# A two-layer transformer on one core: 76 instead of 50 score tiles exponentiated on VectorE, and each engine's instruction order from a table

## The chip, the core and the metric

The kernel runs on one core of a Trainium2 chip. Its engines are TensorE (PE, with its weight loads shown apart as PEld), VectorE (DVE), ScalarE (ACT), GpSimd (POOL) and SyncE (SP, which issues the transfers). They run side by side, each through its own list of instructions in the order in which the program gives them; between engines only semaphores hold order. The metric is the device time of one execution in microseconds (us).

## What is computed

The input x has 2048 rows of 448 numbers in bfloat16. Two layers follow one another with the same weights. Each is an attention block with 16 heads of 28 and then a mixing block with a GELU MLP:

```python
def _A_ref(x, wqkv, wo):
    qkv = (x @ wqkv).reshape(B, S, 3, H, Dh).transpose(2, 0, 3, 1, 4)
    q, k, v = qkv[0], qkv[1], qkv[2]
    scores = jnp.einsum("bhqd,bhkd->bhqk", q, k) * (Dh ** -0.5)
    p = _softmax(scores, axis=-1)
    o = jnp.einsum("bhqk,bhkd->bhqd", p, v)
    return o.transpose(0, 2, 1, 3).reshape(B, S, D) @ wo
def _B_ref(x, w1, w2, w3, w4):
    h = _gelu(_layernorm(x) @ w1)
    # four quarters of h are shifted by 1, -1, 2 and -2 rows
    x1 = x + shifted(h) @ w2
    return x1 + _gelu(_layernorm(x1) @ w3) @ w4
x = A_x
x = x + _A_ref(_layernorm(x), A_wqkv, A_wo)
x = x + _B_ref(_layernorm(x), B_w1, B_w2, B_w3, B_w4)
# ... and both lines once more
```

## The kernel before, in words

**Tiles.** Rows go in 16 tiles of 128. Four heads share the 128 partitions (a head takes 32), so there are four head groups g. A unit u is a block of query rows (512; in the second layer's end also 256). A segment is a unit, a head group and a run of key tiles; `ORDER` (L545) and `UNITS` (L558) lay out 56 of them one after another. For each segment the scores are built transposed, keys on partitions: one score tile is 128 keys by 512 queries of one head and fills one of the eight PSUM banks.

**The exponentials.** Score tiles are put into 821 groups ("grans"), in turn of 3 and 2 tiles: 409 of three, 409 of two and 3 of one. Groups of three lie in banks 0 to 2 or, alternating, groups of two in banks 3 and 4; bank 5 accumulates P·V; banks 6 and 7 (and 0 to 4 outside the attention) serve the rest. For group n, `st_ops` (L1221) issues the score matmuls, four heads on four row strips of the array (L1243). One ACT instruction over all the group's tiles takes the exponential, from PSUM into the buffer `PT` (L1269). Then the matmuls of group n+2 may fill the same banks. `t_pv` (L1280) multiplies P by V, four heads on four column strips (L1318); a column of ones in V gives the softmax denominator. `t_norm` (L1333) takes the sum out of bank 5, in part through a scratch buffer in memory where a segment holds only part of the keys, and divides.

**Tiles on VectorE.** In 50 groups of three the third tile isn't in the ACT instruction: `t_dexp` (L1156) computes its exponential on VectorE in five instructions, by integer arithmetic on the floating-point bits and a cubic: L1159 reads the bank into the integer buffer `t32` (after it the bank is free, event `d1`, for which the third tile's matmul of group n+2 waits), L1166, L1167 and L1168 form the correction in the two halves of `gt`, and L1172 writes the result into one of three `PTD` slots. The PV matmuls of such a tile come up to `DEFER` = 4 key steps later than their neighbours. Which groups do so is said by `OFFL` (L512) and `on_dve` (L1132): every sixth or eighth index in six stretches, if the third tile lies neither in the first nor in the last three key steps of its segment.

**The rest of the work.** K, Q and V of a row chunk come from matmuls on a transposed, normalised copy (`kq_proj` L913, `v_proj` L974). The mixer's first matmul uses a GELU written through tanh, with VectorE before and after ScalarE (`tanh_gelu` L1404); its MLP stores 14 pieces, evacuated by VectorE (L1609), and takes the GELU in few large ACT instructions (L1650), each batch between two loads of ScalarE's function table. The last three tiles take the GELU straight from PSUM (L1606, L1488). A matmul with 128 output columns can be issued whole (L665) or as four of 32 (L668).

**What sets the order.** No order is written out by hand. Every piece of work is a Python generator that yields operations with an estimated duration; `Sched.run` (L319) plays them in a model of the engines, choosing at each step the candidate with the earliest start and the best rank, and appends it to its engine's list. Ranks come from `latest_starts` (L477) of the pass before. `ROUNDS` = 2 passes are followed by two that shift ranks at listed moments by seeded random numbers (`MOVES` L519, `perturb` L455). Where an operation has an alternative engine (`alt`), the model takes it if it ends earlier there, but gives ACT none while the attention runs (`reserve`). A load is modelled as a fixed time from its issue. `keep_pe_busy` (L291) puts filler matmuls on a matrix of ones (line L1686 of the profile) where the model has PE idle, up to 0.8 of a 4 us window. Banks and buffer slots are taken as the model reaches the operation. `Plan` (L47) turns shared buffers into semaphore waits.

Of the kernel before, what the change touches and what calls it, by code (L numbers as in the profile page):

```python
# [17 lines left out]
class _Op:  # L18
    __slots__ = ("eng", "fn", "deps", "sig", "cnt", "waits", "dma", "ekey", "vc", "sem", "t_end", "pos", "every", "oid", "dur", "lft", "lst")

    def __init__(self, eng, fn, dma):
# [16 lines left out]
        self.lst = None  # L38


def _split(acc):
    if isinstance(acc, tuple) and len(acc) == 2 and isinstance(acc[0], tuple):
        return acc
    return acc, None

# [122 lines left out]
class Sched:  # L168
# [8 lines left out]
    def __init__(self, P):  # L177
# [4 lines left out]
        self.pe_mode = None  # L182
        self.act_tab = None
# [8 lines left out]
        self.fill = None  # L192
        self.recent = []
        self.clock = 0.0
        self.plan = None
        self.moves = []
# [3 lines left out]
    def spawn(self, gen, prio=5, order=None, parent=None):  # L200
        self.seq += 1
        if parent is None:
            tid = (self.seq,)
        else:
            parent[7] += 1
            tid = parent[6] + (parent[7],)
        self.tasks.append([prio, self.seq if order is None else order + self.seq * 1e-6, gen, None, None, False, tid, 0, 0, None])

    def rank(self, t):
        if self.plan is None:  # L210
            return (t[0], t[1])
        return (self.plan.get((t[6], t[8]), 1e9), t[1])
# [4 lines left out]
    def _advance(self, t, force=False):  # L217
        changed = False
        while True:
# [39 lines left out]
            elif c == "acq":  # L259
# [22 lines left out]
                t[4] = got  # L282
# [8 lines left out]
    def keep_pe_busy(self, until):  # L291
        if self.fill is None:
            return
        dur, fn, banks, key, reads = self.fill
        while self.cur["pe"] + dur + 0.12 < until:
# [21 lines left out]
            self.pe_mode = "plain"  # L317

    def run(self):  # L319
        P = self.P  # L320
        while True:
            while self.moves and self.clock >= self.moves[0][0]:
                self.perturb(self.moves.pop(0)[1])
# [23 lines left out]
            for t in self.tasks:  # L347
# [5 lines left out]
                for a in kw0.get("alt", ()):  # L353
                    cands.append(a)
# [8 lines left out]
                for ci, (eng, dur, fn, kw) in enumerate(cands):  # L363
# [13 lines left out]
                    if ci > 0 and (self.cur[eng] > ready + 0.05 or eng in self.reserved):  # L377
                        continue
# [57 lines left out]
            op = P.add(eng, fn, reads, writes, kw.get("deps", ()), dma, t_end)  # L436
            self.live.update(k for k in (_split(a)[0] for a in writes) if k[0] == "ps")
            self.live.difference_update(kw.get("last", ()))
            op.oid = (t[6], t[8])
# [15 lines left out]
    def perturb(self, seed):  # L455
        rng = random.Random(seed)
        if rng.random() < 0.2:
            self.SLACK = rng.choice((0.0, 0.06, 0.12, 0.3))
            self.TOL = rng.choice((0.0, 0.5, 1.5, 4.0))
            self.EPS = rng.choice((0.02, 0.05, 0.12))  # L460
        t = self.clock - self.shift
        lo, hi = t - 30.0, t + rng.choice((10.0, 25.0, 50.0, 90.0))
# [1314 lines left out]
```

## Time and profile before

| | before |
|---|---|
| three runs | 1058.69 to 1058.89 us, median 1058.83 |
| profiled execution, first to last instruction | 1059.8 us |
| instructions in it | 22773 |
| first exponential starts, last one's stretch ends | 27.17 us, 1023.12 us |

The profiled execution is one of its own; nothing of it is known beside its span, which is 0.97 us above the median of the runs. A page of the profile gives for each engine the busy time and how many instructions it ran; then the chain of work that ended last, followed back from the last instruction; then groups of instructions, with the line, the engine, the operation, output<-input (partitions x elements and type), the count, and behind the first bar the busy time in us and the mean length of one in ns, behind the second the idle time of the engine just before them and what ended most of it. A row of waits reads: who waited, for whom, us in total, how many times, the longest. A row of windows reads: from:to, its length, busy us (and count) of PE, PEld, DVE, ACT and POOL, the TensorE clock that was granted, the busy share of the transfer engines, GB/s.

### The profile page before, as it was taken

The page shows a single profiled execution, that of the slowest core. Times are in us where ns is not written, and L with a number is a line of the kernel's source. Part 1 is how long each engine was busy: PE and PEld are TensorE (multiplying, and loading weights), DVE is VectorE, ACT ScalarE, POOL GpSimd, SP SyncE. Part 2 cuts the span into 40 slices and gives each one's busy share as a digit, 9 for nine tenths or more (in the row PEclk, how much of TensorE's full clock was granted, in tenths as well). Part 3 has the DMA queues.
Part 4 walks back from the last instruction along what each step waited for, and adds up shares of the span by engine and source line. Part 5 has one row for each costly group of instructions (what it writes and reads, how often), then busy time and mean ns, then how long its engine had stood idle before and what let it go on. Part 6 is the DMA issues. An engine that isn't in the chain of part 4 may idle for free.

```text
span 1059.8 us, 22773 instructions
## 1 busy us (share of the span) xinstructions
PE 1020.3 (96%) x9869; PEld 397.8 (38%) x9883; DVE 744.5 (70%) x1686; ACT 1015.2 (96%) x933; POOL 57.8 (5%) x80
## 2 busy tenths in 40 slices
PE   9999999999999999999999999989999999999998
PEld 5333332333333333333443443323333333434456
DVE  7966579866987547887689657785879645666454
ACT  5999999999999999999999999999999999999983
POOL 2000000100000001010101000000010000010000
PEclk8999999999999999999999999989999999999999
DMA  4243141001101002110111103211010100110000
GB/s 116 63 122 87 36 122 21 2 16 20 21 2 21 1 1 42 36 21 2 21 41 32 29 8 81 81 41 41 21 36 2 20 15 19 21 22 1 15 6 23
DMA packets 70717, 35.14 MB, mean 33 GB/s; under 512 B 56472, under 2 KB 65048, under 8 KB 70616
## 3 DMA queue, kind: packets, MB, share of 16 engines
q1 hardware_dynamic: 70616, 33.68, 13.4%
q8 instruction: 77, 1.26, 0.5%
q14 instruction: 24, 0.20, 0.1%
HBM read 12.70 MB, written 7.08 MB: 19 GB/s over the span
## 4 chain that ended last, share of the span: by engine, by line
ACT 52%; PE 41%; DVE 4%; DMA 1%; issue 1%; SPq 0%; POOLq 0%; POOL 0%; DVEq 0%
ACT PT L1269 45%; PE ps L1243 11%; PE ps L1318 9%; PE ps L665 9%; PE ps L1686 6%; ACT h2T L1650 4%; PE ps L916 3%; PE ps L668 3%; ACT gt L1433 1%; ACT L1650 1%; ACT L1269 1%; DVE kT L925 1%; DMA xT<-xn 1%; DMA wk_raw<-in_A_wqkv_dram 1%; DVE h2T L1609 0%
## 5 line engine op out<-in xcount | busy, mean ns | idle before, releaser
L1269 ACT ACTIVATE PT<-ps 128x1024 bf16<-128x1024 f32 (+1 forms) x821 | 917.2, 1225 | 10.2 <-PE ps L1243 6.4
L1243 PE MATMUL ps<-qT,kT 32*128 32x512 bf16 x1536 | 240.0, 386 | 13.8 <-ACT PT L1269 11.3
L1318 PE MATMUL ps<-PT,vaug 128*32 128x512 bf16 (+1 forms) x2253 | 250.0, 362 | 2.8 <-ACT PT L1269 1.4
L1686 PE MATMUL ps<-ones_bf 128*128 128x256 bf16 x928 | 143.6, 279 | 2.8 <-DVE hot L698 1.1
L1243 PEld LDWEIGHTS ps<-qT,kT 32*128 32x128 bf16 x1536 | 58.6, 91 | 196.1 <-ACT PT L1269 113.7
L665 PE MATMUL ps<-xT,w 112*128 112x512 bf16 (+5 forms) x623 | 129.2, 325 | 0.5 <-DVE h2T L1609 0.2
L1318 PEld LDWEIGHTS ps<-PT,vaug 128*32 128x32 bf16 x2253 | 65.7, 94 | 118.2 <-issue 66.0
L1609 DVE CAST h2T<-ps 128x512 bf16<-128x512 f32 (+2 forms) x126 | 73.5, 583 | 48.2 <-PE ps L665 40.3
L1686 PEld LDWEIGHTS ps<-ones_bf 128*128 128x128 bf16 x928 | 77.4, 99 | 71.3 <-issue 50.8
L1243 PE MATMUL ps<-kT 32*128 32x256 bf16 (+1 forms) x768 | 80.1, 310 | 2.5 <-ACT PT L1269 1.6
L665 PE MATMUL ps<-w,h2T 128*128 128x448 bf16 x327 | 75.1, 354 | 4.8 <-ACT h2T L1650 3.5
L665 PEld LDWEIGHTS ps<-xT,w 112*128 112x128 bf16 (+1 forms) x623 | 50.2, 103 | 53.6 <-issue 27.7
L1159 DVE TENSOR_SCALAR t<-ps 128x512 int32<-128x512 f32 x50 | 34.2, 684 | 34.4 <-PE ps L1243 34.0
L668 PE MATMUL ps<-xT,w 112*32 112x512 bf16 (+4 forms) x612 | 51.5, 337 | 0.0
L916 PE MATMUL ps<-xT,wq_raw 112*32 112x512 bf16 (+1 forms) x576 | 46.8, 367 | 1.9 <-DVE kT L925 0.9
L1243 PEld LDWEIGHTS ps<-kT 32*128 32x128 bf16 x768 | 21.4, 91 | 64.1 <-ACT PT L1269 32.8
L1650 ACT ACTIVATE h2T<-h2T 128x7168 bf16<-128x7168 bf16 (+2 forms) x9 | 44.8, 5010 | 0.1
L1340 DVE STREAM_TRANSPOSE u_sb<-ps 128x512 f32<-128x512 f32 (+1 forms) x24 | 15.0, 626 | 41.2 <-PE ps L1318 41.2
L916 PE MATMUL ps<-xT,wk_raw 112*32 112x512 bf16 (+3 forms) x640 | 41.8, 346 | 0.8 <-DVE vaug L983 0.3
L665 PEld LDWEIGHTS ps<-w,h2T 128*128 128x128 bf16 x327 | 27.9, 98 | 35.1 <-issue 11.7
L1568 POOL TENSOR_TENSOR mst<-mst,neghalf 128x1 f32<-128x1 f32 x32 | 24.3, 762 | 294.6 <-DVE mst L1566 266.5
L815 DVE BATCH_NORM_STATS2 st<-x_res 128x6 f32<-128x448 bf16 x64 | 38.7, 612 | 1.2 <-DMA x_res<-in_A_x_dram 0.6
(145 smaller groups left out, 1065.2 us busy)
## 6 DMA issues: line engine op xcount, KB each, us to landing
uin<-uscr SPq DMA_DIRECT2D x20, 256.0 KB, 2.6
uscr<-u_sb SPq DMA_DIRECT2D x12, 256.0 KB, 2.0
uscr<-uin SPq DMA_DIRECT2D x8, 256.0 KB, 2.0
out_dram<-uin SPq DMA_DIRECT2D x16, 112.0 KB, 1.7
w<-in_B_w_dram SPq DMA_DIRECT2D x4, 392.0 KB, 4.0
x_res<-in_A_x_dram SPq DMA_DIRECT2D x3, 448.0 KB, 8.9
w<-in_B_w_dram SPq DMA_DIRECT2D x2, 448.0 KB, 7.1
w<-in_B_w_dram SPq DMA_DIRECT2D x4, 196.0 KB, 2.8
```

What stands on the lines that cost most here:

```text
L665: return e.matmul(out=dst(0, m), lhsT=lhs(0, m), rhs=rhs, start=start, stop=stop)
L668: return [e.matmul(out=dst(a, min(m, a + 32)), lhsT=lhs(a, min(m, a + 32)), rhs=rhs, start=start, stop=stop, tile_position=(0, a)) for a i ...
L815: yield op("dve", 0.55, lambda e: e.bn_stats(out=st6[:, t, :], in_=x_res[:, t, :]), reads=[("x", t)], writes=[("st6", t)])
L916: yield op("pe", c_mm(nw) + Sched.COLT, lambda e, b=b, fc=fc, rows=rows: [e.matmul(out=ps[32 * j:32 * j + 32, bi(b), 0:nw], lhsT=w[0:rows, ...
L1159: yield op("dve", 0.06 + c_ps(512), lambda e: e.tensor_scalar(out=t32[:, :], in0=ps[:, bk, :], scalar1=0.0, scalar2=65536.0, op0=ALU.max, ...
L1243: yield op("pe", 0.005 if ph == h else 0.012 + W / 2400.0, lambda e, bk=bk, r0=32 * j, g=g, kc=kc, qt=qt, q0=q0, W=W, c0=W * h: e.matmul(o ...
L1269: yield op("act", e_dur(n), lambda e, b0=b0, p0=p0, cnt=cnt: e.activation(out=PT[:, p0:p0 + cnt, :], in_=ps[:, b0:b0 + cnt, :], func=ACT.E ...
L1318: yield op("pe", nt * 0.054 if item in late else 0.004 + nt * 0.0133, lambda e, j=j, rhs=rhs, vs=vs, i=i: e.matmul(out=ps[32 * j:32 * j + ...
L1568: yield op("pool", 0.57, lambda e, t=t: e.tensor_tensor(out=mst[:, t, R3:R3 + 1], in0=mst[:, t, V3E:V3E + 1], in1=neghalf[:, 0:1], op=ALU. ...
L1609: yield op("dve", c_ps(NW), lambda e, fch=fch, b=b: e.tensor_copy(out=h2T[:, fch, hoff:hoff + NW], in_=ps[:, bi(b), 0:NW]), reads=[("ps", ...
L1650: yield op("act", c_act(14 * NW), lambda e, c0=c0, NW=NW: e.activation(out=h2T[:, :, c0:c0 + NW], in_=h2T[:, :, c0:c0 + NW], func=ACT.Gelu ...
L1686: SC.fill = (0.13, lambda e, b: e.matmul(out=ps[:, bi(b), 0:256], lhsT=ones_bf[:, :], rhs=ones_bf[:, :].unsqueeze(1).to_broadcast([128, 2, ...
```

## The change

Five things change.

1. The list of groups whose third tile goes to VectorE is written out: the 50 old ones and 26 more.
2. The planner's order is only a base. It is made without perturbed passes, alternatives or filler. `follow` then takes, for each engine, a table that moves pieces of the base order (take so many, skip so many, a negative skip goes back), and 27 operations that use their other engine; it plays them, each engine strictly in its order, to choose banks and slots by when they become free and to place filler.
3. The model that `follow` plays has the four strips of the array apart (`strip_time`), an SP issue of 0.5 us, and one queue for all loads: each has a latency and a service time and lands after the one before it (`landed`). Loads of the later weights have a `not_before` of 45 us.
4. Buffer names become `Place` objects that get their number only when `follow` reaches them, so views are built late (`lambda`). Which PV matmul of a strip starts or ends an accumulation is counted as they are issued.
5. Some dependences are stated in another way: the scratch use of `h2T` and `w3` in the set-up through `wsqread`; the `tanh_gelu` step before the tanh takes the `gt` halves, one instruction earlier than before; the first correction step of `t_dexp` counts as writing both halves.

The instructions themselves, their shapes and the transfers are the same ones.

```diff
-    OFFL = ((48, 104, 6), (104, 300, 6), (372, 411, 6), (480, 520, 6), (520, 600, 8), (640, 731, 6))
+    DVE_TILES = frozenset((
+        54, 66, 70, 80, 84, 92, 96, 108, 114, 120, 132, 138, 144, 156, 162, 168, 174, 182, 186, 192, 198, 210, 216, 222, 234, 240, 246, 258, 264, 270, 276,
+        284, 288, 294, 300, 302, 314, 324, 372, 378, 386, 390, 396, 402, 414, 476, 480, 492, 496, 498, 506, 510, 552, 560, 570, 580, 632, 648, 654, 660, 668,
+        672, 678, 682, 684, 696, 702, 708, 712, 720, 734, 760, 776, 784, 800, 812))
-    MOVES = [
...
+    ENGINE_ORDER = {
+        "pe": (
+            "0 8 11 4 3 11 2 -3 1 7 1 -3 2 -5 1 -35 2 12 4 -19 1 2 1 37 1 -44 1 -2 1 -2 1 25 2 1 3 -29 1 28 4 4 2 4 3 -21 1 28 1 -9 4 7 1 -8 4 7 3 -9 1 8 1 50 2 "
...
+    OTHER = (
+        42, 44, 61, 62, 63, 66, 110, 117, 127, 133, 136, 154, 165, 169, 171, 177, 189, 195, 222, 238, 248, 274, 346, 9292, 9404, 9515, 9519
+    )
...
+def reorder(ops, text):
+
+    out = []
+    i = 0
+    v = [int(x) for x in text.split()]
+    for k in range(0, len(v), 2):
+        out += ops[i:i + v[k]]
+        i += v[k]
+        if k + 1 < len(v):
+            i += v[k + 1]
+    return out
...
+    def strip_time(self, ready, m, dur, kw):
+
+        sf, tg = list(self.strip_free), list(self.begun)
+        if self.pe_mode is not None and self.pe_mode != m:
+            ready = max([ready] + sf) + self.SW
+            sf = [ready] * 4
+        if m == "plain":
+            end = ready + dur - 0.013
+            return ready, end, end, [end] * 4, tg
+        todo = [(kw["strip"], kw["full"])] if "strip" in kw else [(k, dur - (0.025 if kw.get("mode") == "col4" else 0.026)) for k in range(4)]
...
+    def follow(self, order, other, banks):
+
+        for i in other:
+            op = self.P.all[i]
+            reads, writes, kw = op.spec[2:]
+            op.eng, dur, fn, kw2 = op.alts[0]
+            op.spec = (dur, fn, reads, writes, dict(kw, **kw2))
+        ops, after = self.graph()
+        seq = {}
+        for e in ENGS:
+            mine = [op for op in ops if op.eng == e]
+            seq[e] = reorder(mine, order[e]) if e in order else mine
...
+            if op.dma:
+                new.cur[e] = start + 0.5
+                new.landed = t_end = max(start + kw["lat"], new.landed) + kw["svc"]
+            else:
+                if e == "pe":
+                    new.keep_pe_busy(start)
...
-        for moves in MOVES[:-1]:
-            res = attempt(plan, moves)
-            plan = res[2].latest_starts(res[0])
-        est, P, SC = attempt(plan, MOVES[-1])
+        base = res[2]
+        est, P, SC = base.follow(ENGINE_ORDER, OTHER, MISC)
...
-        def on_dve(n):
+        def may_dve(n):
             if len(grans[n]) < 3:
                 return False
             L, u, g, p, kts, first, last = segs[grans[n][2][0]]
-            return 1 <= grans[n][2][1] <= len(kts) * UNITS[L][u][1] // 4 - 4 and any(a <= n < b and n % m == 0 for (a, b, m) in OFFL)
-
-        DVL = [n for n in range(len(grans)) if on_dve(n)]
-        DVN = {n: k % 3 for k, n in enumerate(DVL)}
+            return 1 <= grans[n][2][1] <= len(kts) * UNITS[L][u][1] // 4 - 4
+
+        DVN = set(n for n in range(len(grans)) if may_dve(n) and n in DVE_TILES)
...
+            def pv(e, i, j, vs, rhs):
+                count[j] += 1
+                return e.matmul(out=ps[32 * j:32 * j + 32, UBK, 0:128 * nt], lhsT=vaug[:, vs, 32 * (4 * g + j):32 * (4 * g + j) + 32],
+                                rhs=rhs(), start=count[j] == 1, stop=count[j] == len(kts), tile_position=(0, 32 * j))
...
-            yield op("dve", 0.07 + nw * 0.00052, lambda e: e.tensor_tensor(out=w, in0=w, in1=half, op=ALU.mult), reads=keys + wk, writes=wk)
...
+            yield op("dve", 0.07 + nw * 0.00052, lambda e: e.tensor_tensor(out=w(), in0=w(), in1=half, op=ALU.mult), reads=keys + wk, writes=wk + tk)
...
-                yield op("sp", 0.1, lambda e, dst=dst, src_=src_: e.dma_start(out=dst, in_=src_), writes=[key], dma=True, dma_time=7.0)
+                yield op("sp", 0.1, lambda e, dst=dst, src_=src_: e.dma_start(out=dst, in_=src_), reads=[("wsqread", 0), ("wsqread", 1)] if key[0] == ("w3",) else [], writes=[key], dma=True, dma_time=7.0, lat=1.7, svc=1.15, not_before=45.0)
```

486 lines of the change are left out of this document (331 added, 155 removed), and 261 rows, old and new, of tables (ENGINE_ORDER, MOVES).

## The prediction

> **What bounds the kernel now.** I read the page's first part and its chain first: they say which engines could set the time. Then the busy time in three stretches (before the first exponential, from the first to the last, after the last), then what ScalarE waits for.
>
> ```profile
> span 1059.8 us, 22773 instructions
> ...
> PE 1020.3 (96%) x9869; PEld 397.8 (38%) x9883; DVE 744.5 (70%) x1686; ACT 1015.2 (96%) x933; POOL 57.8 (5%) x80
> ...
> ACT 52%; PE 41%; DVE 4%; DMA 1%; issue 1%; SPq 0%; POOLq 0%; POOL 0%; DVEq 0%
> ```
> ```profile
> 0.00:27.17 27.17, 24.87 (x288) 14.32 (x289) 19.92 (x84) 14.43 (x20) 7.59 (x20) 0.87 0.43 113
> 27.17:1023.12 995.95, 963.48 (x9266) 361.79 (x9278) 706.04 (x1557) 984.62 (x875) 45.48 (x53) 1.00 0.13 32
> 1023.12:1060.00 36.88, 31.99 (x316) 21.65 (x316) 18.53 (x46) 16.12 (x40) 4.77 (x7) 0.99 0.05 17
> ```
> ```profile
> ACT PT L1269 <- PE ps L1243: 6.4, 14, 1.6
> ACT PT L1269 <- PE ps L1318: 1.3, 2, 0.8
> ```
>
> In the window rows the columns after the length are busy us of PE, PEld, DVE, ACT and POOL, then the granted clock. The middle stretch is 94% of the span, and ScalarE works 984.62 of its 995.95 us: only 11.3 us are idle, of which 7.7 are waits of exponentials for score or PV matmuls. PE looks as full (963.48), but part of that is filler, below. So **ScalarE is the bound of the middle**; head (27.2 us) and tail (36.9 us) are chains in which ScalarE is half idle.
>
> **The change, part by part.** *26 more tiles leave ScalarE.* The new list holds all 50 old groups and 26 more, each with three tiles; its exponential shrinks from 1536 to 1024 columns.
>
> ```profile
> L1269 ACT ACTIVATE PT<-ps 128x1536 bf16<-128x1536 f32 x359 | 525.6, 1464 | 8.1 <-PE ps L1243 5.4 <-PE ps L1318 1.3
> L1269 ACT ACTIVATE PT<-ps 128x1024 bf16<-128x1024 f32 x459 | 467.0, 1042 | 2.0 <-PE ps L1243 1.0
> ```
>
> 1464 - 1042 = 422 ns each, so ScalarE loses 26 x 0.422 = **11.0 us** of work where it is the bound.
>
> *VectorE gains five instructions for each.*
>
> ```profile
> L1172 DVE SCALAR_TENSOR_TENSOR PTD<-t,gt 128x512 uint16<-128x512 int32 x50 | 34.4, 687 | 1.0
> L1167 DVE SCALAR_TENSOR_TENSOR gt<-gt 128x512 f16<-128x512 f16 x50 | 34.4, 687 | 0.9
> L1168 DVE SCALAR_TENSOR_TENSOR gt<-gt 128x512 f16<-128x512 f16 x50 | 34.4, 687 | 1.0
> L1159 DVE TENSOR_SCALAR t<-ps 128x512 int32<-128x512 f32 x50 | 34.2, 684 | 34.4 <-PE ps L1243 34.0
> ...
> L1166 DVE TENSOR_SCALAR gt<-t 128x512 f16<-128x512 uint16 x50 | 21.0, 420 | 1.0
> ```
>
> That is 0.684 + 0.420 + 3 x 0.687 = 3.165 us a tile, 82.3 us for 26, and with the wait in front of the first of them (34.4/50 = 0.69 each) 100 us. VectorE's middle goes from 706 to about 806 of 985 us: 82%. Its cover is its own idle time, 290 us in the middle; I cost it at nothing on the path. The new groups spread so (group n of 821 stands near 27 + 1.213 n us): none before 100 us, 3 up to 200, 1 up to 300, 5 up to 420, 2 up to 560, 3 up to 700, 5 up to 860, 7 after. Three of these stages, each with all engines and then with the filler matmuls (L1686) alone:
>
> ```profile
> 300.00:420.00 120.00, 117.36 (x984) 43.26 (x985) 78.70 (x166) 119.18 (x102) 7.17 (x8) 1.00 0.07 14
> 420.00:560.00 140.00, 134.47 (x1322) 50.54 (x1322) 109.36 (x259) 135.76 (x121) 6.99 (x8) 1.00 0.11 23
> 560.00:700.00 140.00, 134.05 (x1328) 49.55 (x1331) 100.72 (x230) 138.99 (x123) 5.00 (x7) 1.00 0.18 45
> ```
> ```profile
> 300.00:420.00 120.00, 17.40 (x115) 9.68 (x115) 1.00 0.07 14
> 420.00:560.00 140.00, 11.15 (x72) 6.13 (x72) 1.00 0.11 23
> 560.00:700.00 140.00, 6.48 (x45) 3.76 (x45) 1.00 0.18 45
> ```
>
> VectorE in 300 to 420 goes from 78.7 to 78.7 + 5 x 3.165 = 94.5 of about 118 us (80%); 420 to 560, its fullest, to 115.7 of 139 (83%). PE without filler needs 100.0 of 120, 123.3 of 140 and 127.6 of 140. ScalarE gives up 2.1, 0.8 and 1.3 us there, against PE room of 20, 16.7 and 12.4: PE stays below ScalarE, most narrowly in 560 to 700.
>
> *PE.* Each new tile's PV matmul comes apart from its neighbours:
>
> ```profile
> L1686 PE MATMUL ps<-ones_bf 128*128 128x256 bf16 x928 | 143.6, 279 | 2.8 <-DVE hot L698 1.1 <-DVE x_res L1392 0.5 <-DVE hT L1406 0.3
> ...
> L1318 PE MATMUL ps<-PTD,vaug 128*32 128x512 bf16 x49 | 19.2, 392 | 0.0
> ```
>
> Between nothing (beside the other three column strips) and 392 ns (alone): 0 to 10.2 us of PE for 26. The filler, 143.6 us, is the cover, so nothing on the path; were the filler used up, up to those 10.2 us.
>
> *The orders.* No other matmul, transfer or reduction is added. All five engines get a written order (6702, 928, 1809, 76 and 110 entries for PE, ACT, DVE, POOL and SP) in place of the one that a perturbed planner made, and the model behind it now has four array strips, and one queue in which loads land one after another. Such an order can only move waits: the middle's 11.3 us of ScalarE idle time are what it can win at most there. Some come from one place where PE ran at half clock:
>
> ```profile
> 700.00:704.00 4.00, 2.43 (x25) 0.61 (x19) 3.90 (x9) 4.00 (x5) 0.00 (x0) 1.00 0.56 131
> 704.00:706.00 2.00, 2.00 (x8) 0.41 (x7) 2.00 (x6) 1.71 (x2) 0.00 (x0) 0.50 0.00 0
> 706.00:708.00 2.00, 2.00 (x11) 0.84 (x9) 0.69 (x2) 1.29 (x2) 0.00 (x0) 0.50 0.00 0
> 708.00:710.00 2.00, 2.00 (x16) 0.38 (x17) 1.07 (x4) 1.74 (x2) 0.00 (x0) 0.50 0.03 8
> ```
>
> After 4 us in which PE worked only 2.43, the granted clock is 0.50, and ScalarE idles 0.29 + 0.71 + 0.26 = 1.3 us. Against this, the saving itself brings ScalarE closer to PE and VectorE, and waits that its work hid will show. Bounds for the middle's idle time: 11.3 us less (none left) to 11 us more (the whole saving turned to waiting). I take 3 us less, a quarter of what is there: near the end of the present rows, since the stages above keep room.
>
> *Head and tail.* The table of alternatives has 27 entries. Pieces that the trace already shows moved from VectorE to ScalarE:
>
> ```profile
> L923 ACT ACTIVATE qT<-ps,cols 128x512 bf16<-128x512 f32 x4 | 2.8, 688 | 1.8 <-PE ps L916 1.8
> L928 ACT ACTIVATE kT<-ps,cols 128x512 bf16<-128x512 f32 x3 | 2.3, 777 | 5.4 <-PE ps L916 5.3
> L987 ACT ACTIVATE vaug<-ps 128x448 bf16<-128x448 f32 x4 | 2.2, 544 | 0.9 <-PE ps L668 0.9
> ...
> L934 ACT ACTIVATE sq<-qT 128x512 bf16<-128x512 bf16 x1 | 0.6, 630 | 0.0
> L869 ACT ACTIVATE xT<-ps 112x512 bf16<-112x512 bf16 x1 | 0.6, 597 | 0.7 <-PE ps L862 0.7
> ```
>
> These are 13, so up to 14 more pieces of 0.5 to 0.8 us move, 23 of the 27 among the first 346 planned operations and 4 among the last 340: up to 10 us of ScalarE, covered by its 12.7 idle us in the head and 20.8 in the tail. Were one to slip past the first exponential, it would cost its 0.5 to 0.8 us. VectorE, 73% busy in the head, is relieved. Bounds for the head: 3 us less (about four such pieces off its chain) to 2 more; for the tail, where PE idles 36.88 - 31.99 = 4.9 us, 4.9 less to 2 more. I take **1 us less for each**, the low part, since both are chains of single steps.
>
> *Transfers and waits.* SP has 110 entries, as many as it issues now, in another order. Of the transfers only these hold up the chain by more than 5 us (start, length):
>
> ```profile
> 1.82 5.35 DMA wk_raw<-in_A_wqkv_dram
> ...
> 654.67 5.43 DMA xT<-xn
> ```
>
> The first stands as it is. The second could go (up to 5.4 us, inside the bound of the idle time) or a like one come. [...] Bank and slot choice issues nothing.
>
> The sum on the profiled execution: 1059.8 - 11.0 - 3 - 1 - 1 = 1043.8 us. The median of the runs is 1058.83, 0.97 below that span, and carried over this gives 1042.8: I forecast **1043 us**.
>
> **The rivals.**
>
> *PE takes over.* PE is busy 96%, chained at 41%, and from 560 to 700 its own work fills 91%. If score matmuls come late as ScalarE gets faster, most of the 11.0 us turn to idle time. Against: the room per stage above, 9 to 20 times what ScalarE gives up. With 8 of the 11.0 lost and no idle time won: 1058.8 - 3.0 - 2 = 1054 us.
> [...]
>
> *VectorE's queue blocks the scores (slower).* The first VectorE instruction of a tile frees the score bank; PE's next group on that bank waits for it, with all PE work behind. If that instruction stands one instruction (0.69 us) too late, PE loses 0.69 us. The saving of 16.0 us is gone when 16.0/0.69 = 23 of the 76 tiles do so; with 38, half of them, it is 26.2 - 16.0: 1069 us.
>
> ```profile
> DVE t L1159 <- PE ps L1243: 34.0, 27, 3.5
> ```
> ```profile
> who waited for it (us, times):
>   PEld ps L1318: 0.5, 2
>   PEld ps L1686: 0.2, 1
>   PEld ps L862: 0.2, 1
> ```
>
> For it: in 27 of 50 tiles VectorE itself stood waiting at the head of its queue, up to 3.5 us, and everything behind it with it. Against it: what waited for these instructions (second fence) is 0.9 us, and no score matmul is among them.
> [...]
>
> *The search wins more.* All of the middle's idle time goes and the head and tail give 2 each: 1058.8 - 11.0 - 8 to 11.3 - 4 = 1033 to 1036 us.
>
> **How the numbers follow.** Forecast, 1037 to 1050: 0.56. PE takes over, 1050 to 1056.7: 0.15. VectorE blocks, over 1061: 0.15. More, under 1037: 0.11. Within 0.2% (2.1 us, about what a measurement of this kernel can tell from no change): 0.03. So faster 0.82, same 0.03, slower 0.15. The range 1034 to 1059 leaves out the blocked case and the edge of the best one, and takes in head and tail at their bounds and two thirds of the saving lost.
>
> **What would show it.** ScalarE's busy time about 1009 to 1015 (11.0 less, up to 10 more in head and tail); 333 exponentials of 1536 columns and 485 of 1024; 76 of each VectorE step; the first exponential near 26 us, the last ending near 1008. PE takes over: waits of L1269's successor for score matmuls well over 7.7 us. Blocking: score matmuls waiting for the tile's first VectorE instruction by more than 10 us. I am wrong if the middle is not shorter by 10 us or more, or if head or tail move by over 3.

## The result, and the profile after

The kernel after took 1041.94 us (median of four runs, 1038.88 to 1048.76) against 1058.86 for the kernel before (four runs, 1058.69 to 1062.30): ratio 0.9839, 95% interval 0.980 to 0.9878. That is 16.9 us less; 16 were forecast. The same kernel, run six times more beside the last experiments, gave 1041.31 us (1039.50 to 1051.31), ratio 0.9825 (0.9793 to 0.9857). The execution that left the profile took 1048.76 us, the longest of the first four, so its rows show less than the usual gain; the section on the clock says why.

The page of the kernel after, its first lines (busy us, share of the span, instructions), the granted clock in 40 slices, and the chain by engine:

```profile
span 1047.0 us, 23598 instructions
...
PE 974.1 (93%) x10240; PEld 369.3 (35%) x10260; DVE 812.6 (78%) x1809; ACT 1005.5 (96%) x942; POOL 57.7 (6%) x80
...
PEclk9999769999999999999999999999999999999999
...
ACT 79%; PE 19%; DVE 1%; DMA 1%; issue 0%; SPq 0%; DVEq 0%
```

The three stretches of the kernel after: busy us of PE, PEld, DVE, ACT and POOL, then the clock.

```profile
0.00:21.77 21.77, 18.44 (x255) 11.62 (x256) 16.90 (x74) 14.73 (x21) 7.78 (x20) 1.00 0.56 142
21.77:1011.32 989.55, 923.47 (x9659) 335.87 (x9677) 777.69 (x1691) 974.47 (x880) 45.41 (x53) 0.98 0.13 32
1011.32:1047.10 35.78, 32.16 (x329) 21.77 (x327) 18.04 (x45) 16.33 (x43) 4.50 (x7) 1.00 0.06 20
```

Beside the same rows of before: the head is 5.4 us shorter (27.17 to 21.77), the middle 6.4 (995.95 to 989.55), the tail 1.1. In the middle ScalarE works 10.15 us less, as the tiles promised, but is idle 15.1 us instead of 11.3.

The groups of the kernel after that answer to those of the prediction (exponentials by shape, then the filler from the page):

```profile
L1748 ACT ACTIVATE PT<-ps 128x1536 bf16<-128x1536 f32 x333 | 495.8, 1489 | 5.6 <-PE ps L1722 4.4 <-PE ps L1781 0.6
L1748 ACT ACTIVATE PT<-ps 128x1024 bf16<-128x1024 f32 x485 | 494.9, 1064 | 9.0 <-PE ps L1722 6.9 <-PE ps L1781 1.8
```
```profile
L2169 PE MATMUL ps<-ones_bf 128*128 128x256 bf16 x402 | 75.0, 293 | 4.9 <-DVE ones_bf L1158 2.7
```

The counts are those forecast, 333 and 485. The last row is what the prediction never asked about: 402 filler matmuls are left of 928. Without filler PE issues 9838 matmuls instead of 8941, since some 300 with 128 output columns now come as four of 32; so "no other matmul is added" holds for the work and not for the count. It cost little: with the clock held (`more_filler`, below) PE's busy time without filler is about 881 us, against 877 before. And these are ScalarE's waits, then those who waited for the VectorE steps of a tile:

```profile
ACT PT L1748 <- PE ps L1722: 11.3, 20, 1.6
...
ACT PT L1748 <- PE ps L1781: 2.4, 3, 1.4
```
```profile
who waited for it (us, times):
  PEld ps L1722: 4.8, 15
  PEld ps L2169: 2.2, 8
```

Exponentials wait 13.7 us for TensorE (7.7 before). Score matmuls wait 4.8 us for VectorE's tile steps, under the 10 us that the prediction had set for the blocking rival.

**Where the middle lost time: the clock.** Four stretches of 3.41 us from the profile after:

```profile
99.27:102.69 3.42, 1.90 (x13) 0.62 (x14) 3.35 (x6) 3.42 (x4) 0.00 (x0) 1.00 0.33 98
102.69:106.10 3.41, 3.41 (x21) 0.68 (x19) 3.38 (x8) 2.92 (x3) 0.00 (x0) 0.50 0.60 133
...
208.47:211.88 3.41, 1.88 (x22) 0.58 (x21) 3.38 (x7) 3.41 (x5) 0.00 (x0) 1.00 0.00 0
211.88:215.30 3.42, 3.42 (x23) 0.94 (x15) 2.59 (x7) 2.82 (x4) 0.93 (x1) 0.50 0.00 0
```

In the first and third PE works only 1.90 and 1.88 us (55%) at full clock; in the next 3.41 us the granted clock is 0.50, PE is busy throughout, and now ScalarE is idle for 0.5 to 0.6 us of each. Five such dips take 41 us of this profile (the expectations below say six, a miscount); the kernel before had one, of 6.8 us, in its middle. The stretch that holds the longest dip:

```profile
102.69:150.47 47.78, 44.19 (x279) 10.96 (x278) 29.47 (x52) 38.13 (x35) 0.00 (x0) 0.64 0.08 21
```

ScalarE idles 9.65 of these 47.78 us, two thirds of the idle time of the whole middle. The timeline of PE ahead of the first dip (start, length, idle time before it and what ended it):

```profile
100.57 0.39 PE L1722 MATMUL ps<-qT,kT 32*128 32x512 bf16 x3 [0.95 <-ACT PT L1748]
101.49 0.39 PE L1722 MATMUL ps<-qT,kT 32*128 32x512 bf16 x2 [0.53 <-ACT PT L1748]
```

PE waits for exponentials, 0.53 to 0.95 us at a time, with no filler in the gaps. The five dips of this profile are 6.83, 3.41, 23.89, 3.41 and 3.41 us long, whole steps of 3.41 us. The step ahead of each of them had PE 55 to 68% busy, with no gap over 0.96 us.

### The profile page after: what moved, and what is told of

It reads as the page before. It is cut to its first block, busy times and chain, and to the rows that moved or that the text cites. A ratio compares the mean times of both kernels' runs of the same rounds, so it can differ in the third digit from the quotient of the medians.

```text
span 1047.0 us, 23598 instructions
## 1 busy us (share of the span) xinstructions
PE 974.1 (93%) x10240; PEld 369.3 (35%) x10260; DVE 812.6 (78%) x1809; ACT 1005.5 (96%) x942; POOL 57.7 (6%) x80
## 4 chain that ended last, share of the span: by engine, by line
ACT 79%; PE 19%; DVE 1%; DMA 1%; issue 0%; SPq 0%; DVEq 0%
ACT PT L1748 72%; PE ps L1128 6%; PE ps L1722 4%; ACT h2T L2134 4%; PE ps L1781 3%; PE ps L1131 3%; PE ps L1391 1%; ACT gt L1918 1%; PE ps L2169 1%; ACT L2134 1%; DMA wk_raw<-in_A_wqkv_dram 1%; ACT L1748 0%; PE ps L1336 0%; DVE hT L1885 0%; ACT vaug L1461 0%
## 5 line engine op out<-in xcount | busy, mean ns | idle before, releaser
L1748 ACT ACTIVATE PT<-ps 128x1024 bf16<-128x1024 f32 (+1 forms) x821 | 903.0, 1235 | 14.8 <-PE ps L1722 11.3
L1781 PE MATMUL ps<-PT,vaug 128*32 128x512 bf16 (+1 forms) x2221 | 287.8, 369 | 4.1 <-ACT PT L1748 2.6
L1128 PE MATMUL ps<-xT,w 112*128 112x512 bf16 (+6 forms) x483 | 99.2, 318 | 1.4 <-DVE h2T L2094 0.7
L1131 PE MATMUL ps<-xT,w 112*32 112x512 bf16 (+3 forms) x1172 | 90.8, 346 | 0.5 <-DVE h2T L2094 0.4
L2169 PE MATMUL ps<-ones_bf 128*128 128x256 bf16 x402 | 75.0, 293 | 4.9 <-DVE ones_bf L1158 2.7
L1633 DVE TENSOR_SCALAR t<-ps 128x512 int32<-128x512 f32 x76 | 52.2, 687 | 28.4 <-PE ps L1722 27.6
L1131 PE MATMUL ps<-w,h2T 128*32 128x448 bf16 x948 | 60.3, 353 | 2.0 <-ACT h2T L2134 1.6
L1648 DVE SCALAR_TENSOR_TENSOR PTD<-t,gt 128x512 uint16<-128x512 int32 x76 | 52.2, 687 | 3.0 <-PE ps L1781 1.3
L1645 DVE SCALAR_TENSOR_TENSOR gt<-gt 128x512 f16<-128x512 f16 x76 | 52.0, 685 | 1.5
L1644 DVE SCALAR_TENSOR_TENSOR gt<-gt 128x512 f16<-128x512 f16 x76 | 51.9, 683 | 1.3
L1128 PE MATMUL ps<-w,h2T 128*128 128x448 bf16 x211 | 52.1, 355 | 0.0
L2169 PEld LDWEIGHTS ps<-ones_bf 128*128 128x128 bf16 x402 | 33.6, 102 | 43.8 <-issue 19.7
```

Of the source, the lines that this page charges most:

```text
L1128: return e.matmul(out=dst(0, m), lhsT=lhs(0, m), rhs=rhs() if callable(rhs) else rhs, start=start, stop=stop)
L1131: return [e.matmul(out=dst(a, min(m, a + 32)), lhsT=lhs(a, min(m, a + 32)), rhs=rhs() if callable(rhs) else rhs, start=start, stop=stop, t ...
L1633: yield op("dve", 0.06 + c_ps(512), lambda e: e.tensor_scalar(out=t32[:, :], in0=ps[:, bk, :], scalar1=0.0, scalar2=65536.0, op0=ALU.max, ...
L1645: yield op("dve", c_ps(512), lambda e: e.scalar_tensor_tensor(out=half(x), in0=half(f), scalar=EXPB, in1=half(x), op0=ALU.add, op1=ALU.mul ...
L1648: yield op("dve", 0.06 + c_ps(512), lambda e: e.scalar_tensor_tensor(out=PTD[:, to.n, :].bitcast(mybir.dt.uint16), in0=t32[:, :], scalar=2 ...
L1748: yield op("act", e_dur(n), lambda e, b0=b0, p0=p0, cnt=cnt: e.activation(out=PT[:, p0:p0 + cnt, :], in_=ps[:, b0:b0 + cnt, :], func=ACT.E ...
```

## The experiments

Theory: 26 tiles take 11 us off ScalarE, the head gained 5 to 6 us from pieces handed to ScalarE, and thin filler lets the clock fall and gives some of it back. Rivals: the orders alone made the middle's gain; the loads' order made the head's; the dips have nothing to do with filler.

### Filler: more, none, and less in the kernel before

`more_filler` changes two constants of keep_pe_busy: how busy a window may get, and the smallest gap that is filled (in both places where it stands). All five orders and the tiles stay, and 606 filler matmuls come out instead of 402:

```diff
-    TARGET = 0.8
+    TARGET = 2.0
...
-        while self.cur["pe"] + dur + 0.12 < until:
+        while self.cur["pe"] + dur + 0.02 < until:
```

> The kernel after with the same five orders and the same 76 tiles, but with 606 filler matmuls instead of 402: filler is put into every gap of TensorE of 0.15 us and more, whatever its recent load. Theory 1 (the profiled execution after lost time to the granted clock, which fell to 0.50 in six stretches of 41 us together, because TensorE's waits there were no longer filled): fewer and shorter dips, a mean clock of 0.993 or more in all runs, a span near the best one seen after, 1037 us, with a spread between runs under 4 us. Rival (the filler is harmless to leave out, and more of it only delays the score matmuls that it stands ahead of): mean clock and spread as after (0.980 to 0.993, 1037 to 1047 us) or the time longer by some us at an unchanged clock.

Measured: 1040.15 us (1039.96 to 1041.26), ratio 0.9823 (0.9804 to 0.9842), clock 0.993 to 0.997. Its middle, from the windows:

```profile
21.68:1002.52 980.84, 931.12 (x9847) 348.87 (x9865) 777.85 (x1691) 973.27 (x880) 45.40 (x53) 1.00 0.14 32
```

The theory's marks on clock and spread hold. With the clock held, ScalarE idles 7.6 us in the middle instead of 15.1, and the middle is 15.1 us shorter than before's. But no run came under 1039.96, a span of 1038.2 where 1037 was expected: the filler itself seems to have a price, below.

`after_no_filler` and `before_thin` leave filler out when the instructions are written, so that no order and no plan changes:

```diff
+        skip = set(op for op in self.fills if not op.waits and not op.sig)
         for op in self.ops[eng_name]:
+            if op in skip:
+                continue
```

In `after_no_filler` that is 316 of the 402; in `before_thin` the ones whose number leaves a remainder of 0, 2 or 4 by seven stay as well, so that 431 of 928 are left.

> The kernel after with the same orders, and every filler matmul left out that carries no wait of its own. The filler's product is used by nothing. Theory 1 (missing filler lets the clock fall): more stretches at 0.50, a mean clock under 0.97 and a time well over 1050 us: the profiled execution after, with 41 us of dips, had 9.65 us of idle time on ScalarE in 48 us of them, so each further 41 us of dips costs about 6 to 8 us. Rival (the dips are not the filler's doing): mean clock 0.980 to 0.993 as after, time 1038 to 1048 us or a little less, since fewer matmuls stand ahead of the scores.

Measured: 1091.12 us (1088.03 to 1094.38), ratio 1.0303 (1.0272 to 1.0334), clock 0.913 to 0.925. The granted clock of its page:

```profile
PEclk9997779879987899995999999998699999879999
```

These 316 filler matmuls are worth about 49 us: more than the whole change brings. The expected price of a dip (6 to 8 us for 41 us of them) was about half of what came: this profile has 164 us at 0.50, 123 more than that of after, and its span is 41 us longer.

> The kernel before with its own order and its 50 tiles, and 497 of its 928 filler matmuls left out (every second one or so of those that carry no wait), which leaves 431, about as many as the kernel after has. The filler's product is used by nothing. Theory 1: the clock falls here too, in more than the one dip of 6.8 us that the profile before showed; mean clock 0.97 to 0.99, time 1062 to 1070 us and a spread of several us where before agrees within 0.2. Rival (the dips come from the new orders or from the 76 tiles, not from the number of fillers): 1058 to 1060 us with at most one dip.

Measured: 1061.67 us (1058.14 to 1065.59, ten runs), ratio 1.0024 (1.0005 to 1.0043), clock 0.979 to 0.994 where before has 0.990 to 1.000. Its profile has five dips between 100 and 1050 us. So the dips come to the kernel before as well when its filler is thinned to after's number. Yet the time, in between the two marks, rises by only 2 to 2.5 us. That isn't the price of the dips alone: at the same mean clock (the line for before in the next part, extended below its lowest clock of 0.990) these ten runs lie 2 to 6 us under the kernel before, and the middle of this profile (992.47 us) is 3.5 us shorter than before's in spite of its dips. So filler seems to have a price in the kernel before too, about 4 us for these 497, which thinning gives back. The number of fillers is a part of the cause of the dips; that the gaps left in the kernel after lie closer together may be another, which no run shows.

### The same kernel again: time against clock

> The kernel after, unchanged, for more runs beside the others on one chip. Theory: a spread of 8 us and more that goes with the mean clock (0.98 to 0.995, about 0.75 us for each 0.001), a median of 1041 to 1044 us; dips begin in the same few stretches of steps in every profile, and which of them do differs from run to run. Rival (the spread of the first four runs was chance or the chip's): all within 2 us.

Measured: 1041.31 us, with 1039.50 at a clock of 0.993 and 1051.31 at 0.976; spread 11.8 us. The middle of its profiled execution (1042.16 us, clock 0.989, four dips, ScalarE idle for 9.9 us) is nearer to the usual run than the one above:

```profile
21.32:1004.74 983.42, 920.86 (x9679) 335.75 (x9677) 777.96 (x1691) 973.56 (x880) 45.40 (x53) 0.99 0.14 32
```

A straight line through the ten runs of after (time against mean clock) falls by 0.70 us for each 0.001 of clock and leaves a scatter of 0.3 us: the clock explains nearly the whole spread. The same line for the 49 runs of before beside the experiments (1056.39 to 1063.54) has 0.65 and leaves 0.7. At one clock, 0.995, the lines give 1060.4 for before and 1038.1 for after, the second a little beyond after's highest clock: **the change is worth about 22 us at an equal clock**, and after runs at a lower one (0.976 to 0.993), which takes back some 2 to 5 of them in the medians. About 4 of the 22 may be the price of filler that after no longer has, by `before_thin`; no run takes that part alone. `more_filler`'s 1040.1 at 0.997 lies 3.4 us over after's line, and its run at 0.993 lies 1.8 to 2.4 us over after's two runs at that clock: the price of 204 more fillers; that it is paid where they stand ahead of score matmuls is a guess that no run shows. So it wins steadiness (1.3 us of spread instead of 12), hardly time.

Which stretches bring a dip? I cut fourteen profiles into the 3.41 us steps of their clock and took PE's busy share in each step between the first and the last exponential that ran at full clock. Under 0.65, 34 of 45 steps were followed by a dip; from 0.65 to 0.75, 19 of 97; from 0.75 to 0.85, 4 of 320; above, none of some 3500. The steps begin at other places in the two profiles of after (their dips start at 102.69 and at 100.52 us), so one thin spot can fall into one step in one run and be split between two in another. The busy share alone does not sort these steps. Of the eleven steps under 0.65 without a dip, ten have a single gap of 1.2 to 1.9 us, while in 30 of the 34 with a dip no gap is over 0.97. So one long gap is not what brought a dip in these profiles; what else counts beside the share stays open.

### Smaller filler, and scores issued twice

> The kernel more_filler with filler matmuls of 128 columns instead of 256, which fit into gaps from 0.1 us: 1153 of them instead of 606. Theory 1 (what is left of the dips, two in more_filler's profile, comes from gaps too short for the filler): a mean clock of 0.998 or more in every run and 1038 to 1039.5 us. Rival (TensorE's many small instructions delay the scores behind them, or the dips that are left have another cause): 1040 us or more, or the same clock of 0.993 to 0.997.

`small_filler` changes one line of `more_filler`:

```diff
-            SC.fill = (0.13, lambda e, b: e.matmul(out=ps[:, bi(b), 0:256], lhsT=ones_bf[:, :], rhs=ones_bf[:, :].unsqueeze(1).to_broadcast([128, 2, 128]), start=True, stop=True),
+            SC.fill = (0.076, lambda e, b: e.matmul(out=ps[:, bi(b), 0:128], lhsT=ones_bf[:, :], rhs=ones_bf[:, :], start=True, stop=True),
```

Measured: 1046.97 us (1043.38 to 1049.48), clock 0.982 to 0.990. The theory is wrong: the profile has five dips, and they fell in stretches (101, 125, 203, 463 and 968 us) where the thin spots of the other profiles lie too. Why 1153 small matmuls held the clock less well than 606 large ones (0.993 to 0.997) was not settled.

`scores_twice` fills those spots without a free PSUM bank, in the 72 steps listed in `TWICE`:

```diff
-                        rhs=qt[r0:r0 + 32, g, q0:q0 + W], start=True, stop=True, tile_position=(r0, 0)),
+                        rhs=qt[r0:r0 + 32, g, q0:q0 + W], start=True, stop=True, tile_position=(r0, 0)) for _ in range(2 if n in TWICE else 1)],
```

> The kernel more_filler, with the score matmuls of 72 of the 818 steps issued twice in a row into the same place (the second writes the same values again). The steps are those of the stretches in which the profiles after and more_filler both have 3.41 us with TensorE busy under 0.70 of the time, and in which its waits for ScalarE, 0.36 to 0.53 us each, hold no filler, because no PSUM bank is free there (steps 64 to 73, 80 to 92, 120 to 128, 153 to 161, 239 to 246, 350 to 356, 611 to 619, 662 to 668). Theory (the clock falls after a 3.41 us stretch in which TensorE is busy under some 0.63 to 0.70 of the time, wherever the 3.41 us happen to begin in that run): no dip in these steps in any run, a mean clock of 0.997 or more in all six, 1037 to 1040 us, spread under 2.5 us; the doubled matmuls lie in TensorE's own waits and cost nothing. Rival 1 (they delay the exponentials): the same clock and 1042 us or more. Rival 2 (the share of busy time is not what the clock goes by): dips at the same places as before, mean clock down to 0.99.

Measured: 1046.82 us (five runs, 1045.74 to 1049.84), clock 1.000 in three of them and 0.998 and 0.996 in the others, so one under the 0.997 of the theory. Three of the stretches in `scores_twice`, and the same in `more_filler`:

```profile
97.00:104.00 7.00, 6.53 (x61) 1.80 (x58) 6.60 (x13) 6.88 (x7) 0.00 (x0) 1.00 0.35 78
114.00:120.00 6.00, 5.38 (x63) 1.48 (x59) 4.67 (x10) 5.89 (x7) 0.00 (x0) 1.00 0.01 3
198.00:206.00 8.00, 7.05 (x67) 2.10 (x65) 7.59 (x18) 7.41 (x8) 1.17 (x2) 1.00 0.00 0
```
```profile
97.00:104.00 7.00, 5.48 (x47) 1.80 (x46) 6.30 (x12) 6.97 (x10) 0.00 (x0) 1.00 0.31 67
114.00:120.00 6.00, 4.58 (x46) 1.39 (x45) 4.50 (x10) 6.00 (x7) 0.00 (x0) 0.86 0.00 0
198.00:206.00 8.00, 6.52 (x55) 2.42 (x55) 7.79 (x17) 8.00 (x9) 1.37 (x2) 1.00 0.00 0
```

PE is busier by 0.5 to 1.1 us in each; the dip in the second is gone (clock 0.86 to 1.00), and this profile has none at all before its last microsecond. So rival 2, dips at the same places, did not come. The doubled matmuls raise the busy share and shorten the gaps at once, so the run doesn't tell which of the two the clock goes by. ScalarE is idle 0.8 us more over the three rows, and the whole takes 6.7 us longer than `more_filler`. Rival 1 is right on the price: in this profile exponentials wait 8.8 us for scores, in that of `more_filler` 6.2. No version here beats `more_filler` and after clearly.

### The tiles

`tiles_back_mf` is `more_filler` with 26 tiles back on ScalarE:

```diff
+        DVN.difference_update(gone)
+        late.clear()
+        late.update((grans[n][2], n) for n in DVN)
+        seqs["dve"] = [o for o in seqs["dve"] if not (o[0][-1][0] == "t_dexp" and o[0][-1][1] in gone)]
...
+                seqs["pe"].remove(mine[0])
+                seqs["pe"].insert(seqs["pe"].index(mates[-1]) + 1, mine[0])
```

> The kernel more_filler (the orders after, filler in every gap, 1040.2 us, last exponential 980.8 us after the first) with 26 of its 76 tiles of the score back on ScalarE, so that 50 are left on VectorE; 130 VectorE instructions go, 26 exponentials grow from 1024 to 1536 columns, and the 26 tiles' value matmuls stand beside those of the same key step; all else keeps its order. Theory (the tiles themselves give 26 x 0.422 us = 11 us of the middle's 15): first to last exponential 992 us, the whole 1051 us. Rival 1 (TensorE had taken over as the bound, the tiles were worth little and the orders gave the rest): at most 985 us and 1044 us. Rival 2 (the orders fit 76 tiles only, and with 50 the longer exponentials make the scores late as well): 998 us or more and 1057 us or more, with ScalarE's idle time in front of the exponentials grown by 6 us and more.

Measured: 1061.64 us (1057.02 to 1067.79), clock 0.984 to 0.998. The exponentials (from the page) of `tiles_back_mf`, of `more_filler` and of before:

```profile
L1756 ACT ACTIVATE PT<-ps 128x1024 bf16<-128x1024 f32 (+1 forms) x821 | 914.0, 1246 | 13.9 <-PE ps L1789 6.8
```
```profile
L1748 ACT ACTIVATE PT<-ps 128x1024 bf16<-128x1024 f32 (+1 forms) x821 | 901.6, 1235 | 7.3 <-PE ps L1722 6.2
```
```profile
L1269 ACT ACTIVATE PT<-ps 128x1024 bf16<-128x1024 f32 (+1 forms) x821 | 917.2, 1225 | 10.2 <-PE ps L1243 6.4
```

The middle of `tiles_back_mf`:

```profile
22.20:1022.10 999.90, 947.52 (x9959) 359.37 (x9977) 703.76 (x1561) 985.72 (x880) 44.19 (x53) 0.99 0.14 31
```

It is 999.9 us instead of 980.8. Of these 19 us, 12.4 are the exponentials themselves (914.0 - 901.6): the 26 tiles, near the 11.0 worked out. The other 6.6 are new idle time: exponentials now wait 6.8 us for value matmuls (L1789), and 0.2 in `more_filler`. Rival 2's marks are met, so the order fits its 76 tiles, though the place I gave to the 26 tiles' value matmuls may have made part of that wait.

### The head: alternates and loads

`alternates_back` takes the 27 alternates back, in the kernel after; `alternates_back_mf` does so in `more_filler` (was[o] is the engine that an operation is written for, begin[o] its planned start):

```diff
+        for e in ("act", "dve"):
+            for o in [o for o in seqs[e] if was[o] != e]:
+                seqs[e].remove(o)
+                into = seqs[was[o]]
+                k = 0
+                while k < len(into) and begin[into[k]] < begin[o]:
+                    k += 1
+                into.insert(k, o)
```

> The kernel after with its 27 alternates undone: the 23 operations of the head and 4 of the tail that the table hands to the other engine (transposed tiles, biases of keys and queries, the ones columns of the values to ScalarE; some to VectorE) go back to the engine that they are written for, each put into that engine's order at its planned start; everything else keeps its order. Theory (the head's 5.4 us came from ScalarE taking work off VectorE there): the first exponential starts near 26 to 27 us instead of 21.8, the middle stays as it is, and the whole takes 4 to 8 us longer than after. Rival (the head gained from the order of loads and projections, not from the other engine): the first exponential stays within 1 us of 21.8 and the whole within 2 us of after.

> The kernel more_filler with the 27 alternates undone, as in the run before, which took 17 us longer than after, but at a mean clock of 0.979 and with seven dips. Theory 1 (most of the 17 us are the alternates themselves: the first exponential came 7.2 us later there, and the first 60 exponentials took 9.4 us longer): at a clock of 0.993 or more still 1050 to 1052 us, first exponential at 28 to 29 us, and the further 3 us in the first 60 exponentials. Rival (the dips made most of it): under 1046 us once filler holds the clock.

Measured: 1058.95 us (1049.79 to 1063.88, clock 0.976 to 0.992) and 1055.88 us (1050.66 to 1062.62, clock 0.981 to 0.995). The first expectation, 4 to 8 us, was too low. At one clock the loss is 9 to 12 us in both: 1049.79 and 1050.92 at 0.992 against after's 1040.34 and 1040.45, 1051.65 at 0.993 against `more_filler`'s 1041.26, and the ten runs of `alternates_back` lie 9.6 to 12.4 us over after's line. So theory 1 of the second holds, and dips made up the rest of the 17 us. How many exponentials have begun by 96.00 us, before the first of the new tiles at step 70 (busy us and count of their line, in before, after, `alternates_back_mf`):

```profile
0.00:96.00 96.00, 67.63 (x60) 0.96 0.38 98
```
```profile
0.00:96.00 96.00, 73.18 (x65) 1.00 0.49 124
```
```profile
0.00:96.00 96.00, 64.12 (x57) 1.00 0.46 109
```

Five exponentials more than before; without the alternates three fewer. In `alternates_back_mf` the head and the longest wait of an exponential are:

```profile
0.00:27.98 27.98, 25.25 (x311) 16.75 (x313) 20.74 (x81) 8.84 (x11) 7.61 (x20) 1.00 0.43 110
```
```profile
ACT PT L1756 <- PE ps L1730: 24.7, 19, 14.6
```

ScalarE works 8.84 us of the head and then waits 14.6 for the first scores, instead of working 14.73. One caution: the kernel before had 13 such pieces on ScalarE already, and here none is left, so the run shows that the new order needs them, not that the 14 further ones alone made the gain.

`loads_back_mf` gives the loads the program's own order:

```diff
+        at = [k for k, o in enumerate(seqs["sp"]) if o[0][-1] == ("t_setup2",)]
+        by = {op.oid: k for k, op in enumerate(base.P.ops["sp"])}
+        for k, o in zip(at, sorted((seqs["sp"][k] for k in at), key=lambda o: by[o])):
+            seqs["sp"][k] = o
```

> The kernel more_filler with the loads of x's later chunks and of the weights of values, mixer and output in the order in which the program asks for them (values' weights first, then chunks 1, 2, 3, and so on), in the places that the searched order gives to loads; stores and all other engines keep their orders. Theory (the order of the loads hardly matters where it stands; the head's 5.4 us are the alternates'): within 1 us of more_filler, first exponential at 21.7 to 22.5 us. Rival (the loads modelled as one shared queue gave the head its gain): the first exponential 2 us or more later and the whole 1042 us or more.

Measured: 1044.55 us (1041.50 to 1047.44), clock 0.989 to 0.995; first exponential at 22.48 us, 0.8 later, and 65 exponentials by 96 us, as many as in `more_filler`. The median is 4.4 us over `more_filler`'s, so the theory's 1 us is missed and the rival's mark on the time is met, though not its mark on the first exponential. Near one clock the difference is smaller: 1041.50 at 0.995 stands between `more_filler`'s 1041.26 at 0.993 and 1040.28 at 0.997, but 1043.19 at 0.993 is 1.9 us over the first of these. So the searched order of the loads gave 0 to 2 us where it was tried, and the rest goes with the clock (0.989 to 0.995 instead of 0.993 to 0.997). Whether the order of the loads also brought the lower clock, four runs can't say.

### Without the tables

```diff
-        est, P, SC = base.follow(ENGINE_ORDER, OTHER, MISC)
+        est, P, SC = attempt(plan, True)
```

> The kernel after with its 76 tiles, without its order tables, its alternates and its second pass: every engine works in the order that the planner itself comes to, with filler as in the kernel before. Theory (the tables are what makes the 76 tiles pay; tiles_back_mf lost 19 us for 26 tiles, of which 12.4 us were ScalarE's busy time and 6.6 us new idle time): first exponential near 28 us, ScalarE's busy time as after (1004 us), but 30 us and more of idle time in the middle, so over 1065 us, slower than the kernel before. Rival (the tables give only the head's 5 to 7 us): 1047 to 1052 us.

> The same kernel without tables, with the 26 tiles back on ScalarE, so 50 tiles. Theory 1 (a tile is worth its 0.422 us of ScalarE only where the scores behind it come in time, which the planner's own order does not see to): under 6 us slower than no_tables_76. Theory 2 (the tiles give their 11 us in any order, since ScalarE bounds the kernel): 10 to 13 us slower than no_tables_76, with ScalarE's busy time up by 12 us and its idle time unchanged.

`no_tables_50` has this line too, and its set of VectorE tiles is the one without the 26.

Measured: 1098.47 us (ratio 1.035, 1.0324 to 1.0375) and 1102.86 (1.0394, 1.0369 to 1.0419). Middle and tail of the first, then of the second:

```profile
22.64:1047.72 1025.08, 988.13 (x9195) 377.17 (x9194) 769.91 (x1702) 976.73 (x875) 49.90 (x59) 0.99 0.13 30
1047.72:1097.50 49.78, 43.54 (x503) 29.71 (x502) 24.15 (x63) 14.26 (x39) 4.73 (x7) 1.00 0.07 22
```
```profile
23.02:1062.07 1039.05, 1000.16 (x9746) 390.12 (x9745) 705.84 (x1587) 987.61 (x875) 48.54 (x59) 0.99 0.13 30
1062.07:1102.00 39.93, 33.29 (x357) 21.73 (x357) 18.13 (x47) 14.41 (x38) 4.42 (x7) 0.98 0.05 15
```

The difference of 4.4 us would suit theory 1, but the rows give theory 2 for the middle: ScalarE's work falls by 10.9 us (987.61 to 976.73) and its idle time stays (51.4 and 48.4), so the tiles pay there even in a bad order; the 76 then lose 9.9 us in the tail (39.93 to 49.78), where this order leaves more work. And the tables matter more than the tiles: with the same 76 tiles ScalarE idles 48.4 us in the middle without them, and 7.6 to 15.1 with them. That is no price against before, whose own order was a searched one too (11.3 us idle). One mark was missed: the first exponentials come at 22.6 and 23.0 us and not near 28, early like after's, without any alternate on ScalarE. Yet only 54 and 53 have begun by 96 us, fewer than in the kernel before. So an early first exponential needs no alternates, and it is no sign of a fast head.

## Why the prediction was right, and where it was wrong

- **Tiles, 11.0 us: right.** ScalarE's work in the middle fell by 10.15 us in the profiled execution (with two more table loads in it); 26 tiles put back cost 12.4 us of exponentials.
- **Its own signs of being wrong** were both met in the profiled execution: the middle is 6.4 us shorter and not 10 or more, and the head moved by 5.4 and not within 3. In the second profile of after the middle passes (12.5 us shorter) and the head, 5.9, does not. So the time came out while the account of the head, and of the middle in part, did not.
- **The middle's idle time, 3 us less: right at a held clock only.** It was 11.3; `more_filler` shows 7.6, after 15.1 in the profiled execution and 9.9 in the second. The step that failed is the sentence that the filler "is the cover": I counted it as spare room for matmuls and forgot that it holds the clock (0.976 to 0.993 in after, 0.913 to 0.925 without 316 of its fillers). I had quoted the place in before where 4 us with PE 2.43 us busy are followed by a clock of 0.50, and did not ask how much filler a planner would still find room for.
- **Head, 1 us less: mis-sized.** It is 5.4 us less, outside my own bounds (3 less to 2 more), and at the 61st exponential 5.9 (96.09 to 90.15). I priced each piece that leaves VectorE singly; taking all 27 back costs 9 to 12 us at equal clock, though that also takes away the 13 that before had.
- **Tail, 1 us less: right** (36.88 to 35.78).
- **ScalarE's busy time, "about 1009 to 1015":** a slip of its own sum, since 1015.2 less 11.0, and up to 10 more, is 1004.2 to 1014.2. It is 1005.5.
- **The sum** of 16 came out by luck, because two misses cancelled: 4 to 5 us too little for the head, and some for the middle (in part perhaps the price of the old filler), against 2 to 5 us lost to the clock in the medians.
- **PE takes over:** its mark, exponentials waiting well over 7.7 us for score matmuls, was met in the profiled execution (11.3, and 13.7 with value matmuls) and not in `more_filler` (6.2, the row below). PE did not run short of room; it ran at a clock of 0.50 for 41 us of that profile.

```profile
ACT PT L1748 <- PE ps L1722: 6.2, 14, 1.1
```

- **VectorE's queue blocks the scores:** no; 4.8 us in 15 waits.
- **The bound of 0.2% for what can be told apart** was too fine: the three runs of before that I had agreed within 0.2 us, the fourth lay 3.4 us higher, and the 49 later ones spread over 7.

## What to carry to other kernels

Filler matmuls are not only free room (leaving out 316 of them cost the kernel after 49 us): before a change that packs the schedule, count what it leaves of them and look for stretches of a few microseconds in which TensorE falls under three quarters busy (here 53 of 142 such steps were followed by a dip). Filler can have a price of its own, too (here, as estimated above, about 4 us for 497 in before and 1.8 to 3.4 for 204 in `more_filler`). Compare variants at equal mean clock, or a line of time against clock over many runs, before a microsecond is given to an edit. In a head that is a chain over several engines, pieces that move to an idle engine add up (here taking 27 back cost 9 to 12 us at equal clock), and the count of main-loop instructions begun by a fixed time shows it better than the first one's start (here 54 by 96 us after a first one at 22.64 in `no_tables_76`, 60 after one at 27.17 in before).

## What the runs showed of the hardware that I had not expected

- The granted clock fell to 0.50 for one or more steps of 3.41 us after a single step with PE 55 to 79% busy (the nine dips of the two profiles of after), without any gap over 0.96 us in it. Each 0.001 of mean clock, 2.1 us at 0.50, cost the kernel after 0.70 us, so one step of 3.41 us about 1.1.
- The mean duration of an exponential grew from 1464 and 1042 ns to 1489 and 1064 while their busy time fell (917.2 to 903.0 us): an instruction overlaps its successor here (by 0.12 us before and 0.15 after on the mean), and start to start of neighbours stayed at 1.33 and 0.90 us in both (medians). The difference of the two, 0.43 us, is the price of a tile here; a mean duration alone is not.
